# Seven block products for four of the eight tile pairs in batch 2's input stage, with VectorE's work there in a new order

## The chip, the core and the metric

One core of a Trainium2 chip runs the whole program: no other core takes part, and there is one launch. The metric is the device time of one execution in microseconds (us). The kernel before was run three times: 207.71, 206.24 and 207.14, median 207.14. One execution was recorded by the hardware profiler; its own time is 205.84 us, and its span, from the first to the last instruction of the trace, is 204.10 us.

The engines are TensorE (PE in the profile, its weight loads PEld), VectorE (DVE), ScalarE (ACT), GpSimd (POOL) and SyncE (SP), which here only issues transfers. An issue of a transfer stands on the queue of the engine that makes it.

## The reference

Four batches of attention with eight heads, 768 tokens and 64 columns a head feed a layer of two matrix products. Each query sees the keys within 15 positions of its own, and 24 summaries: of each block of 32 keys the maximum, of each block of 32 values the mean, with log 32 added to their score.

```python
k_sum = k.reshape(B, H, nb, block, D).max(axis=3)      # B, H, S, D = 4, 8, 768, 64; block = 32
v_sum = v.reshape(B, H, nb, block, D).mean(axis=3)
scores_l = scale * q @ k.T                             # kept where |i - j| < 16
scores_s = scale * q @ k_sum.T + log(block)
a = softmax(concat([scores_l, scores_s]))
x = (a @ concat([v, v_sum])) -> (3072, 512)
h = x @ w_in                                           # w_in: 512 x 2048
g = h / (1 + exp(-1.702 * h))
out = g @ w_out                                        # w_out: 2048 x 512, out: 3072 x 512, float32
```

## The kernel before, in words

**Engines and order.** Each engine runs its instructions in the order in which the program writes them; the framework sets the semaphores between engines. So the order of the calls in the program is the order of each queue. All helpers record through one wrapper, so nearly every instruction of the profile has line 28, and tiles are told apart by their names.

**Stages.** A batch has 768 tokens, two halves of 384. Its *input stage* multiplies x (transposed, `xTT`, tile name `xT`) by w_in and applies the gelu on ScalarE into `gT`, 16 tiles of 128 of the 2048 middle columns by 768 tokens. Its *output stage* multiplies `gT` by w_out and writes tokens in groups of 128. Batch 0 goes through a lead of its own (the calls from line 920 on) and `ff_in`, `ff_out`; batches 1 and 2 through the loop at line 1124; batch 3 through the code from line 1171.

**Plain input products.** A tile is two halves of 384 columns; each is four matmuls of 128 x 128 by 384 (`ff_step`). The loop takes tiles in pairs j and j + 8, in the order `order2`. A pair is 16 matmuls.

**Seven block products.** The matrices are cut in 2 x 2 blocks, and sums of blocks replace eight block products by seven, in Strassen's manner. For the output stages of batches 1 to 3 `product(b, t, what)` (line 775) does this: `gs` holds four sums of blocks of `gT` (`g_sums`, line 683), `ws` four sums of blocks of w_out (`w_sum`); each `what` is eight matmuls of 256 columns that share a weight sum, and `keep_it` (799), `give` (806) and `store` (816) hold, add and write the results. The variable `seq` gives the order of the products. In the last group the last copy is cut in two, a VectorE half stored on SyncE's queue and a ScalarE half stored on its own.

For the input stage only batch 3 does this, for six of its eight pairs (`PLAIN = 2`). `win_sum` (716) makes four sums `wsi` of blocks of w_in, each 128 x 2048, and `x_sums` (725) four of x. `win_sum` is called four times on VectorE at the start of batch 2's input stage (line 1129). For a pair, `ff_product` (739) does product 1 to 7 of two matmuls each, `ff_copy` (757) moves partial sums between banks: "a" a VectorE copy of bank A into bank C, "s" a ScalarE copy of bank E, "b" and "c" VectorE sums of bank A with "s" into bank B and into bank E. `ff_gelu` (771) ends a bank. The table `steps` (1198) says in which of a pair's slots each is called; a new pair starts every seven slots, so neighbouring pairs overlap. The banks come from `last_bank` (733): three of A, one of B, two of C and two of E.

**The next batch's attention, beside.** During the input stage of batch b the keys, queries and values of batch b + 1 are made ready. Transfers: SyncE transposes keys (`xk`, line 567) and queries (`xq`, 574) by DMA, in pairs of heads; GpSimd issues the loads (`load_batch`, 246; `load_turned`, 123, called at 1146 for the next queries, behind a small GpSimd copy `gate2` that waits for x). `value_rows` (1077) sums the values' blocks: 48 small matmuls (`vsum`, 280) into `ps_vs`, then `block_sums` (304) on VectorE, then transfers to `vw`. `rest_k` (578), for each pair of heads, takes the maxima of the key blocks on VectorE into `ks`, then copies the halos (`key_halos`, 355) and the rows of maxima (`key_rows`, 349) into `kx`. During the output stage `beside` (1057) takes from the table `plan` (1038) by slot: "s" scores and their exponential, "m" mask, "v" values (601, with `norm`, 625: one reciprocal and one product for each of two banks), "d" the transposition of x by DMA (`dx`, 639, on SyncE's queue).

**The sums gs around batch 2.** After each pair of tiles in batch 1 and 2, `g_sums` makes the four sums of that pair on VectorE; two of the last pair's come after the first product of the output stage.

**The lead.** For batch 0, keys and queries are turned on TensorE. `q_turn` (401) writes the turned queries of two pairs of heads into two parts of one bank, and `q_copy` (407) takes them out, one pair on VectorE and one on ScalarE. `idle(n)` (298) is n matmuls whose results nobody reads. `v_sum` (483, first called at 970) sums the value blocks.

Of the kernel before, what the change touches and what calls it, by code (L numbers as in the profile page):

```python
# [35 lines left out]
def kernel(  # L36
# [311 lines left out]

    def key_rows(p, s, ks, eng=dve, j0=0):
# [228 lines left out]
    def rest_k(p, s, eng=dve):  # L578
        ks = attp.tile([128, nb], BF16, name="ks", tag="ks")
# [21 lines left out]
    def values(b, half, g):  # L601
# [19 lines left out]
        x2[g] = attp.tile([128, 2, JH, 2, D], F16, name="x2", tag="x2", bufs=4)  # L621
        for i in range(2):
            norm(x2[g][:, :, :, i].rearrange("p h j d -> p j h d") if b else x2[g][:, i], pvs[i])

    def norm(x, pv):
        rc = attp.tile([128, 2, JH, 1], F32, name="rc", tag="rc")
# [89 lines left out]
    def win_sum(what):  # L716
# [6 lines left out]
        dve.tensor_tensor(out=wsi[what], in0=a, in1=b_, op=op)  # L723
# [51 lines left out]
    def product(b, t, what):  # L775
# [40 lines left out]
        def store(o, tok, cols=slice(0, d_model)):  # L816
            r0 = b * S + tok
            sp.dma_start(out=out[r0:r0 + 128, cols], in_=now[t, o][:, cols])
# [117 lines left out]
    s_bias(1)  # L936
    q_turn(0)
# [4 lines left out]
    idle(6)  # L942
# [32 lines left out]
    av_edges(0)  # L975
# [148 lines left out]
    for b in range(1, B - 1):  # L1124
        nxt = b + 1 < B
        s = (b + 1) % 2
        if b == B - 2:
            for w in range(4):
                win_sum(w)
        for n in range(0, NT, 2):  # L1130
            if n == 0:
                ff_open(order2[0:4], (lambda: tx(1, 1)) if b == 1 else None)
            elif n == 2:
                for nt in order2[0:4]:
                    ff_one(1, nt)
                g_sums(0)
                g_sums(1)
            else:
# [3 lines left out]
                g_sums(n // 2, dve, (0, 1) if n + 2 == NT else (0, 1, 2, 3))  # L1142
            if nxt:
                if n == 0 and b > 1:
                    pool.tensor_copy(out=gate2, in_=xTT[1][1][:, 1, 0:1])
                    load_turned(q, b + 1, qb2, "qb")
                if n // 2 == 1:
                    value_rows(s)
                if n // 2 == 2 * b:
                    xq(0, s)  # L1150
                    xq(1, s)
                if n // 2 in (2, 3, 4, 5):
                    rest_k(n // 2 - 2, s)
        if nxt:
            exp_soon()
            beside(b + 1, -1)
        i = 0
        for t, what in seq:
            product(b, t, what)
            if i == 0:  # L1160
                g_sums(NT // 2 - 1, dve, (2, 3))
            if nxt:
# [9 lines left out]
    for ab in (True, False):  # L1172
        plast[ab] = ctx.enter_context(tc.tile_pool(name=f"plast{ab:d}", bufs=2, space=bass.MemoryType.PSUM))
    b, n = B - 1, NT // 2
    PLAIN = 2

    def plain(nt, half, tag):
        ph = last_bank(tag, "ph")[:, 0:HALF]
        ff_step(ph, half, nt)
        gelu(half, nt, ph)  # L1180

    def ff_do(j, what):
        if isinstance(what, int):
            ff_product(j, what)
        elif what in "asbc":
            ff_copy(j, what)
        elif what == "g":
            g_sums(j, pool, (0, 1))
        else:
            ff_gelu(j, what)  # L1190

    for i, tag in enumerate("CCEEAAA"):
# [3 lines left out]
        if i in (5, 6):  # L1196
            g_sums(0, pool, (0, 1) if i == 5 else (2, 3))
    steps = {0: [1, "a"], 1: [5, "s"], 9: [7, "c"], 10: [3], 4: [2], 5: [6, "b"], 13: [4],
             6: ["C"], 11: ["B"], 12: ["E"], 14: ["A"], 15: ["g"]}
# [20 lines left out]
    q_ = slice(PLAIN, n)  # L1220
# [35 lines left out]
```

## Time and profile before

| what | value |
|---|---|
| runs (us) | 207.71, 206.24, 207.14; median 207.14 |
| the profiled execution (us) | 205.84, its span 204.10 |
| granted TensorE clock, mean over the span | 0.995 |
| instructions in the span | 5864 |
| HBM read, written | 27.26 MB, 6.29 MB |
| largest group | 416 matmuls of `ph`, 128x384: 70.2 us |
| second largest | 104 ScalarE gelus into `gT`, 128x384: 49.8 us, 491 ns each |

The profile's page is read from the top. The first part gives each engine's busy time and its share of the span; the chain of waits follows the end of the program back to what released each step, and so tells which engine the time is made of; the groups of instructions give the mean duration of one. A view of stretches of time cuts these by stage, and the timeline gives single instructions: their start in us from the start of the span, their duration, engine, operation, output and inputs, and in brackets the idle time ahead of them with what ended it. The stages of the profiled execution, by the first and last matmuls of each: batch 1's input stage from 74.2 to 96.05, its output stage to 118.6; batch 2's input stage to 140.05 and output stage to 162.6; batch 3's to 183.4 and 204.1.

### The profile page before, as it was taken

The page shows a single profiled execution, that of the slowest core. Times are in us where ns is not written, and L with a number is a line of the kernel's source. Part 1 is how long each engine was busy: PE and PEld are TensorE (multiplying, and loading weights), DVE is VectorE, ACT ScalarE, POOL GpSimd, SP SyncE. Part 2 cuts the span into 40 slices and gives each one's busy share as a digit, 9 for nine tenths or more (in the row PEclk, how much of TensorE's full clock was granted, in tenths as well). Part 3 has the DMA queues.
Part 4 walks back from the last instruction along what each step waited for, and adds up shares of the span by engine and source line. Part 5 has one row for each costly group of instructions (what it writes and reads, how often), then busy time and mean ns, then how long its engine had stood idle before and what let it go on. Part 6 is the DMA issues. An engine that isn't in the chain of part 4 may idle for free.

```text
span 204.1 us, 5864 instructions
## 1 busy us (share of the span) xinstructions
PE 197.2 (97%) x2364; PEld 137.0 (67%) x2364; DVE 139.1 (68%) x387; ACT 125.9 (62%) x241; POOL 92.1 (45%) x143
## 2 busy tenths in 40 slices
PE   7999999999999999999999999999999999999991
PEld 6567554556664666566888866657888865578881
DVE  6666876585854974897767698996759446757221
ACT  4686874549777617777771546778651578982220
POOL 7965489446999691002965054000000029990000
PEclk9999999999999999999999999999999999999997
DMA  5999999999999999999999979995024920000232
GB/s 171 173 166 204 208 209 219 180 154 240 111 155 150 189 181 126 168 177 104 145 206 132 178 125 152 125 245 131 17 89 111 158 94 3 0 0 3 103 118 89
DMA packets 96138, 28.13 MB, mean 138 GB/s; under 512 B 83680, under 2 KB 93296, under 8 KB 96112
## 3 DMA queue, kind: packets, MB, share of 16 engines
q0 software_dynamic: 69648, 13.24, 85.4%
q1 hardware_dynamic: 26320, 14.46, 34.0%
q8 instruction: 18, 0.29, 0.6%
q14 instruction: 8, 0.07, 0.1%
q10 hardware_dynamic: 144, 0.07, 0.1%
HBM read 27.26 MB, written 6.29 MB: 164 GB/s over the span
## 4 chain that ended last, share of the span: by engine, by line
PE 92%; ACT 3%; DMA 2%; DVE 1%; issue 0%; SPq 0%; DVEq 0%
PE ph L28 33%; PE poA L28 16%; PE po L28 11%; PE poB L28 8%; PE ps_av L28 4%; PE ps_s L28 4%; PE poC L28 4%; PE phA L28 4%; DMA gT<-in_k_dram 2%; PE ps_t L28 1%; PE ps_x L28 1%; PE phB L28 1%; PE phC L28 1%; ACT a_sb L28 1%; PE ps_vt L28 1%; PE phE L28 1%
## 5 line engine op out<-in xcount | busy, mean ns | idle before, releaser
L28 PE MATMUL ph<-xT,w_in_sb 128*128 128x384 f16 x416 | 70.2, 326 | 0.1
L28 PEld LDWEIGHTS <-w_in_sb 128*128 128x128 f16 x452 | 43.7, 98 | 27.8 <-issue 0.2
L28 ACT ACTIVATE gT<-ph 128x384 f16<-128x384 f32 x104 | 49.8, 491 | 18.5 <-PE ph L28 18.2
L28 PEld LDWEIGHTS <-gT 128*128 128x128 f16 x312 | 28.8, 98 | 11.0
L28 ACT ACTIVATE a_sb<-ps_s 128x768 bf16<-128x768 f32 (+1 forms) x32 | 25.0, 826 | 10.8 <-PE ps_s L28 10.8
L28 PEld LDWEIGHTS <-gs 128*128 128x128 f16 x288 | 27.7, 98 | 3.4
L28 POOL DMA_DIRECT2D vw<-in_v_dram x36 | 24.5, 701 | 11.5 <-DMA kb<-in_k_dram 4.2
L28 POOL TENSOR_TENSOR gs<-gT 128x384 f16<-128x384 f16 x9 | 8.2, 909 | 42.4 <-ACT gT L28 42.4
L28 PE MATMUL po<-w_out_sb,gT 128*128 128x512 f16 x96 | 23.6, 380 | 0.0
L28 DVE TENSOR_TENSOR a_sb<-a_sb,mk 128x768 bf16<-128x768 bf16 x28 | 14.9, 554 | 6.5 <-ACT a_sb L28 5.9
L28 PE MATMUL poA<-ws,gs 128*128 128x256 f16 x144 | 18.7, 273 | 0.0
L28 DVE TENSOR_TENSOR x<-ps_av,rc 128x384 f16<-128x384 f32 x32 | 17.8, 557 | 1.1
L28 DVE TENSOR_TENSOR gs<-gT 128x384 f16<-128x384 f16 (+1 forms) x34 | 13.4, 393 | 7.2 <-ACT gT L28 6.9
L28 POOL DMA_DIRECT2D qb<-in_q_dram x16 | 15.1, 961 | 1.8 <-DMA w_in_sb<-in_moe_w_in_dram 1.3
L28 PEld LDWEIGHTS <-kx 64*128 64x128 bf16 (+1 forms) x372 | 9.4, 95 | 6.8 <-issue 4.4
L28 POOL DMA_DIRECT2D kb<-in_k_dram x14 | 13.6, 991 | 0.3 <-issue 0.3
L28 DVE TENSOR_REDUCE ks<-kx 128x24 bf16<-128x768 bf16 x12 | 11.4, 948 | 3.4 <-ACT kx L28 3.2
L28 ACT ACT_TABLE_LOAD x10 | 12.8, 1283 | 1.0 <-PEq L1240 0.8
L28 ACT ACTIVATE osb<-poA 128x256 f32<-128x256 f32 (+1 forms) x9 | 3.3, 372 | 16.2 <-PE poA L28 12.7
L28 ACT ACTIVATE s<-poA 128x256 f32<-128x256 f32 x11 | 4.2, 385 | 11.2 <-PE poA L28 11.2
L28 PEld LDWEIGHTS <-a_sb 128*64 128x64 bf16 (+2 forms) x400 | 7.9, 108 | 2.8 <-issue 1.3
L28 PE MATMUL poA<-w_out_sb,gT 128*128 128x256 f16 x72 | 9.4, 273 | 0.0
(119 smaller groups left out, 282.3 us busy)
## 6 DMA issues: line engine op xcount, KB each, us to landing
out_dram<-osb SPq DMA_DIRECT2D x22, 256.0 KB, 3.7
kb<-in_k_dram POOLq DMA_DIRECT2D x14, 192.0 KB, 7.1
qb<-in_q_dram POOLq DMA_DIRECT2D x12, 192.0 KB, 9.9
vw<-in_v_dram POOLq DMA_DIRECT2D x36, 64.0 KB, 5.5
w_out_sb<-in_moe_w_out_dram POOLq DMA_DIRECT2D x4, 512.0 KB, 13.0
w_in_sb<-in_moe_w_in_dram POOLq DMA_DIRECT2D x3, 512.0 KB, 12.6
vw<-vs SPq DMA_DIRECT2D x6, 198.0 KB, 5.8
gT<-in_k_dram SPq DMA_DIRECT2D x2, 384.0 KB, 3.6
```

Of the source, the lines that this page charges most:

```text
L28: r = f(*a, **kw)
```

## The change

- **Batch 2's input stage** (`in_seven`, line 1215 of the changed kernel) takes four pairs (j = 0 to 3) in the plain way and four (j = 4 to 7) by seven block products, with the same `steps`. One half of tiles 3 and 11 is put between the last pair's products. The second of the four pairs starts its product 1 and copy "a" at slot 2 of the stage, five slots sooner than its place. The banks A (three) and B (one) are now opened for batches 2 and 3 alike, C and E for each stage by itself; batch 2's output stage uses A and B, and a new pool `psb2` for the attention beside it. The block sums of values use the two E banks.
- **Sums of w_in.** Sums 0 and 2 go to GpSimd, after the output products of batch 1 that have slots 9 and 10; sums 1 and 3 stay on VectorE at the start of batch 2.
- **Keys of batch 3.** The maxima are taken for two pairs of heads at a time (`key_max`): the first two pairs in one piece after `value_rows`, the other two in three parts, after slots 10, 17 and 24. Their halos (`key_halos2`) and rows (`key_rows2`) go to GpSimd. In batch 1's input stage the same is done on VectorE, two pairs at a time.
- **Sums of gT in batch 2.** Sums 0 and 1 of pairs 0 and 1 in one VectorE operation each; of pair 2 on GpSimd; sums 2 and 3 of pairs 0 and 1 on GpSimd after slots 3 and 6; sums 0 and 1 of pairs 4 to 6 on GpSimd by `steps`; of the last pair and of pair 3 on VectorE at the end. Sums 2 and 3 of pairs 2 to 7 are two VectorE operations of 128 x 2304 (`sums23`), after the first and the second output product. In batch 1 the sums of two pairs at a time are one operation each.
- **Queries of batch 3** (`xq`) are transposed after slot 8.
- **Values** of batches 2 and 3: one reciprocal and one product for the two banks.
- **The lead.** Each turned query has a bank of its own; two idle matmuls ahead of the first `q_turn` replace six behind it; the first value sums and the first own and edge products of values come sooner, and `s_bias(3)` later.
- **The tail.** The last copy is one ScalarE operation and one store on its queue.

The core of the diff:

```diff
     def vsum(s):
 
-        if s == 1 and not vs_ps[0]:
+        if plast:
+            ps = [last_bank("E", "ps_vs") for e in range(2)]
...
+    def key_max(g, s, part=0, parts=1):
+
+        flat = kxs[s].rearrange("p i t c -> p (i t c)")
+        o, n = 2 * g * NQ * 128, 2 * NJ // parts
+        if part == 0:
+            ks_of[g] = attp.tile([128, 2, nb], BF16, name="ks", tag="ks2", bufs=2)
+        dve.tensor_reduce(out=ks_of[g].rearrange("p i (j e n) -> p (i j) e n", e=2, n=2)[:, part * n:(part + 1) * n],
+                          in_=at(flat, o + 256 * n * part, [[256, n], [192, 2], [block, 2], [1, block]]),
+                          axis=AX.X, op=ALU.max)
...
+    def key_halos2(g, s, eng):
+        flat = kxs[s].rearrange("p i t c -> p (i t c)")
+        o, n = 2 * g * NQ * 128, 2 * NJ
+        eng.tensor_copy(out=at(flat, o + 256 + 96, [[256 * NJ, 2], [256, NJ - 1], [1, 16]]),
...
     def q_turn(p):
-        if p % 2 == 0:
-            st["Q2"] = pturn.tile([128, 1024], BF16, name="ps_q", tag="turn")
-        st["Q", p] = st["Q2"][:, p % 2 * HALF:p % 2 * HALF + HALF]
+        st["Q", p] = pturn.tile([128, 1024], BF16, name="ps_q", tag="turn")[:, 0:HALF]
         turn_plain(st["Q", p], qe[:, 2 * p:2 * p + 2])
...
+            pv = ps.rearrange("p (i c) -> p i c", i=2)[:, :, 0:390].rearrange("p i (n c) -> p i n c", c=D + 1)
+            rc = attp.tile([128, 2, 2 * JH, 1], F32, name="rc", tag="rc2", bufs=2)
+            dve.reciprocal(out=rc, in_=pv[..., D:D + 1])
+            dve.tensor_mul(x2[g].rearrange("p h j i d -> p i (h j) d"), pv[..., 0:D],
+                           rc.to_broadcast([128, 2, 2 * JH, D]))
+            return
...
-    def g_sums(j, eng=dve, which=(0, 1, 2, 3)):
-
-        a1, a2 = gTb[:, j], gTb[:, j + NT // 2]
+    def g_sums(j, eng=dve, which=(0, 1, 2, 3), n=1):
+
+        j1, j2 = slice(j, j + n), slice(j + NT // 2, j + NT // 2 + n)
+        a1, a2 = gTb[:, j1], gTb[:, j2]
         l, r = slice(0, HALF), slice(HALF, S)
         for w in which:
-            a, b_, op = {0: (a1[:, r], a2[:, r], ALU.add), 1: (gs[:, 0, j], a1[:, l], ALU.subtract),
-                         2: (a1[:, l], a1[:, r], ALU.subtract), 3: (a2[:, l], gs[:, 1, j], ALU.subtract)}[w]
-            eng.tensor_tensor(out=gs[:, w, j], in0=a, in1=b_, op=op)
+            a, b_, op = {0: (a1[:, :, r], a2[:, :, r], ALU.add), 1: (gs[:, 0, j1], a1[:, :, l], ALU.subtract),
+                         2: (a1[:, :, l], a1[:, :, r], ALU.subtract),
+                         3: (a2[:, :, l], gs[:, 1, j1], ALU.subtract)}[w]
+            eng.tensor_tensor(out=gs[:, w, j1], in0=a, in1=b_, op=op)
 
     N1 = d_model // 2
...
-    def win_sum(what):
+    def win_sum(what, eng=dve):
...
+    def open_last(stack, b, tags):
+        for tag, n in tags:
+            plast[tag] = stack.enter_context(tc.tile_pool(name=f"last{tag}{b}", bufs=n, space=bass.MemoryType.PSUM))
+
     def last_bank(tag, name):
-        return plast[tag in "AB"].tile([128, 512], F32, name=name, tag="last" + tag,
-                                       bufs={"A": 3, "E": 2, "B": 1, "C": 2}[tag])
+        return plast[tag].tile([128, 512], F32, name=name, tag="last" + tag)
...
             now[t, bank] = (last_bank("B" if bank == "A" and t == 2 else {"A": "A", "B": "E", "C": "C"}[bank],
                                       "po" + bank) if b + 1 == B
-                            else pmm.tile([128, 512], F32, name="po" + bank, tag="mm"))
+                            else last_bank("B" if bank == "B" else "A", "po" + bank) if b + 2 == B
+                      else pmm.tile([128, 512], F32, name="po" + bank, tag="mm"))
         po = now[t, bank][:, 0:N1]
         for i in range(n):
...
         elif last:
-            for c, eng, queue in ((slice(0, 128), dve, sp), (slice(128, N1), act, act)):
-                copy(eng, now[t, "o2"][:, c], po[:, c])
-                queue.dma_start(out=out[b * S + HALF + t * 128:b * S + HALF + t * 128 + 128, c],
-                                in_=now[t, "o2"][:, c])
+            give("o2", lo, None)
+            store("o2", HALF + t * 128, lo, act)
         else:
...
     s_bias(1)
+    idle(2)
     q_turn(0)
     q_turn(1)
     q_copy(0, dve)
     q_copy(1, act)
     k_max(0)
-    idle(6)
...
     k_max(3)
     s_bias(2)
-    s_bias(3)
     s_own(2)
-    s_own(3)
     s_edges(2)
     s_exp(2)
+    s_bias(3)
+    v_sum((0,))
+    s_own(3)
     s_edges(3)
     s_exp(3)
-    v_sum((0,))
+    av_own(0)
+    av_edges(0)
     v_sum((1,))
     v_copy((0, 1), dve)
-    av_own(0)
     av_own(1)
-    av_edges(0)
...
+    def sums23(j0):
+        q_ = slice(j0, NT // 2)
+        yield dve.tensor_tensor(out=gs[:, 2, q_], in0=gTb[:, q_, 0:HALF], in1=gTb[:, q_, HALF:S], op=ALU.subtract)
+        yield dve.tensor_tensor(out=gs[:, 3, q_], in0=gTb[:, j0 + NT // 2:NT, 0:HALF], in1=gs[:, 1, q_],
+                                op=ALU.subtract)
...
+    def in_plain():
+        s = 0
...
-                g_sums(1)
+                g_sums(0, n=2)
...
+                if n // 2 in (3, 5):
+                    g_sums(n // 2 - 1, n=2)
...
+            if n // 2 in (2, 4):
+                rest_k2(n // 4 - 1, s)
...
+    def in_seven(b, first):
+
+        n, s = NT // 2, (b + 1) % 2
+        for w in (1, 3):
+            win_sum(w)
+        pool.tensor_copy(out=gate2, in_=xTT[1][1][:, 1, 0:1])
+        load_turned(q, b + 1, qb2, "qb")
+        for i, tag in enumerate("CCEEAAAB"):
+            plain((0, n, 1, n + 1)[i % 4], i // 4, tag)
+            if i == 3:
+                x_sums()
+        value_rows(s)
+        key_halos2(0, s, pool)
+        key_max(0, s)
+        key_rows2(0, s, pool)
+        for i, tag in enumerate("CCAA"):
+            plain(2 + n * (i % 2), i // 2, tag)
+        g_sums(0, dve, (0, 1), 2)
+        for i in range(2):
+            plain(3 + n * i, 0, "E")
+        g_sums(2, pool, (0, 1))
+        key_halos2(1, s, pool)
+        for slot in range(7 * (n - first)):
+            for j in range(first, n):
+                at_ = slot - 7 * (j - first)
+                if j == first + 1 and at_ in (0, -5):
+                    at_ = -1 if at_ == 0 else 0
+                for what in steps.get(at_, ()):
+                    ff_do(j, what)
+            if slot in (3, 6):
+                g_sums(slot // 3 - 1, pool, (2, 3))
+            if slot in (10, 17, 24):
+                key_max(1, s, slot // 7 - 1, 3)
+            if slot == 8:
+                xq(0, s)
+                xq(1, s)
+            if slot == 24:
+                key_rows2(1, s, pool)
+        last = n - 1
+        ff_do(last - 1, "A")
+        plain(3, 1, "C")
+        ff_do(last, 7)
+        ff_do(last, "c")
+        ff_do(last, 3)
+        ff_do(last - 1, "g")
+        ff_do(last, "B")
+        ff_do(last, "E")
+        plain(3 + n, 1, "E")
+        ff_do(last, 4)
+        ff_do(last, "A")
+        g_sums(last, dve, (0, 1))
+        g_sums(3, dve, (0, 1))
+
+    for b in range(1, B - 1):
+        seven = b == B - 2
+        if seven:
+            mid.close()
+            open_last(ctx, b, (("A", 3), ("B", 1)))
+            with ExitStack() as banks:
+                open_last(banks, b, (("C", 2), ("E", 2)))
+                in_seven(b, 4)
+            mid = ExitStack()
+            psb = mid.enter_context(tc.tile_pool(name="psb2", bufs=2, space=bass.MemoryType.PSUM))
+            bulk = sums23(2)
+        else:
+            in_plain()
+        exp_soon()
...
             if i == 0:
-                g_sums(NT // 2 - 1, dve, (2, 3))
-            if nxt:
-                beside(b + 1, i)
+                if seven:
+                    beside(b + 1, -1)
+                else:
+                    g_sums(NT // 2 - 1, dve, (2, 3))
+            beside(b + 1, i)
             i += 1
-            if nxt and b + 2 < B:
+            if b + 2 < B:
...
                     load_batch(b + 2)
                 if i in (16, 18):
                     xk(i // 2 - 8, b % 2)
+                if i in (9, 10):
+                    win_sum(2 * (i - 9), pool)
 
...
+    open_last(ctx, B - 1, (("C", 2), ("E", 2)))
```

More of the change, by code (lines that the diff above doesn't have):

```diff
@@ L280, in vsum @@
     def vsum(s):
-        if s == 1 and not vs_ps[0]:
+        if plast:
+            ps = [last_bank("E", "ps_vs") for e in range(2)]
+        elif s == 1 and not vs_ps[0]:
             ps = [pmm.tile([128, 512], F32, name="ps_vs", tag="mm") for e in range(2)]
@@ L625, in norm @@
     def norm(x, pv):
[L626 removed]
+        rc = attp.tile([128, 2, JH, 1], F32, name="rc", tag="rc", bufs=4)
         dve.reciprocal(out=rc, in_=pv[..., D:D + 1])
@@ L722, in win_sum @@
                      2: (a11, a21, ALU.subtract), 3: (a12, wsi[1], ALU.subtract)}[what]
-        dve.tensor_tensor(out=wsi[what], in0=a, in1=b_, op=op)
+        eng.tensor_tensor(out=wsi[what], in0=a, in1=b_, op=op)
     def x_sums():
@@ L731, with plain, ff_do @@
     plast = {}
+    def open_last(stack, b, tags):
+        for tag, n in tags:
+            plast[tag] = stack.enter_context(tc.tile_pool(name=f"last{tag}{b}", bufs=n, space=bass.MemoryType.PSUM))
     def last_bank(tag, name):
-        return plast[tag in "AB"].tile([128, 512], F32, name=name, tag="last" + tag,
-                                       bufs={"A": 3, "E": 2, "B": 1, "C": 2}[tag])
+        return plast[tag].tile([128, 512], F32, name=name, tag="last" + tag)
+    def plain(nt, half, tag):
+        ph = last_bank(tag, "ph")[:, 0:HALF]
+        ff_step(ph, half, nt)
+        gelu(half, nt, ph)
+    def ff_do(j, what):
+        if isinstance(what, int):
+            ff_product(j, what)
+        elif what in "asbc":
+            ff_copy(j, what)
+        elif what == "g":
+            g_sums(j, pool, (0, 1))
+        else:
+            ff_gelu(j, what)
+    steps = {0: [1, "a"], 1: [5, "s"], 9: [7, "c"], 10: [3], 4: [2], 5: [6, "b"], 13: [4],
+             6: ["C"], 11: ["B"], 12: ["E"], 14: ["A"], 15: ["g"]}
     ff_now = {}
@@ L814, in product, with store @@
         last = b == B - 1 and t == JH - 1
-        def store(o, tok, cols=slice(0, d_model)):
+        def store(o, tok, cols=slice(0, d_model), queue=sp):
             r0 = b * S + tok
-            sp.dma_start(out=out[r0:r0 + 128, cols], in_=now[t, o][:, cols])
+            queue.dma_start(out=out[r0:r0 + 128, cols], in_=now[t, o][:, cols])
             if not last:
@@ L1123 @@
     halves[0] = True
[L1124 to L1129, printed above, removed]
+    def sums23(j0):
[5 more added lines that the diff above has]
+        s = 0
         for n in range(0, NT, 2):
             if n == 0:
-                ff_open(order2[0:4], (lambda: tx(1, 1)) if b == 1 else None)
+                ff_open(order2[0:4], lambda: tx(1, 1))
             elif n == 2:
@@ L1141 @@
                         ff_one(half, nt)
-                g_sums(n // 2, dve, (0, 1) if n + 2 == NT else (0, 1, 2, 3))
-            if nxt:
[L1144 to L1153, printed above, removed]
@@ new lines @@
+    for b in range(1, B - 1):
[12 more added lines that the diff above has]
+        exp_soon()
+        if not seven:
@@ L1219 @@
     product(b, 2, 1)
-    q_ = slice(PLAIN, n)
-    dve.tensor_tensor(out=gs[:, 2, q_], in0=gTb[:, q_, 0:HALF], in1=gTb[:, q_, HALF:S], op=ALU.subtract)
-    dve.tensor_tensor(out=gs[:, 3, q_], in0=gTb[:, PLAIN + n:2 * n, 0:HALF], in1=gs[:, 1, q_], op=ALU.subtract)
+    for _ in sums23(PLAIN):
+        pass
     for t in range(JH):
```

47 lines of the change are left out of this document (25 added, 22 removed).

## The prediction

> **What bounds the kernel now.** I read the page's busy shares and its chain of waits, then the busy times by stage, then the timeline at the places that the change touches, last the transfers of single issues.
>
> ```profile
> PE 197.2 (97%) x2364; PEld 137.0 (67%) x2364; DVE 139.1 (68%) x387; ACT 125.9 (62%) x241; POOL 92.1 (45%) x143
> PE 92%; ACT 3%; DMA 2%; DVE 1%; issue 0%; SPq 0%; DVEq 0%
> 0.00:19.50 19.50, 17.10 (x343) 13.12 (x344) 12.47 (x42) 12.60 (x21) 14.81 (x23) 1.00 1.44 178
> 118.60:140.05 21.45, 21.45 (x181) 12.78 (x180) 19.58 (x57) 15.25 (x32) 5.04 (x5) 1.00 1.48 174
> 162.60:183.40 20.80, 20.74 (x135) 12.93 (x133) 12.03 (x23) 17.22 (x40) 15.72 (x18) 1.00 0.09 29
> ```
>
> The last three rows are stages: length, then busy time of PE, weight loads, DVE, ACT and POOL, then clock, DMA share, GB/s. TensorE is 92% of the chain. It stands 2.4 us in the first 19.5 and not at all in batch 2's input stage (118.60 to 140.05), where VectorE's 19.58 us are work that nobody waits for. So an edit gains what it takes from TensorE, and loses what it makes TensorE wait.
>
> **Products.** A plain pair is 16 matmuls, a pair by seven products 14. Four pairs: 8 matmuls fewer, each 15.71 / 96 = 0.164 us: -1.31, all on the path.
>
> ```profile
> 118.61 5.20 PE ph L28 x32
> 123.81 0.53 PE ps_vs L28 x48
> 124.34 15.71 PE ph L28 x96
> 169.21 0.57 DVE L28 TENSOR_TENSOR phB<-phA,vw 128x384 f32<-128x384 f32 x1 [1.05 <-PE phA L28]
> 169.69 0.56 DVE L28 COPY phC<-phA 128x384 f32<-128x384 f32 x1
> 169.83 0.48 PE L28 MATMUL phA<-vw,kx 128*128 128x384 f16 x2
> 170.35 0.57 DVE L28 TENSOR_TENSOR phE<-phA,vw 128x384 f32<-128x384 f32 x1
> ```
>
> Batch 3 shows the new coupling: product 7 starts (169.83) 0.05 after VectorE's sum (169.21 + 0.57), so TensorE now depends on three VectorE operations a pair, 1.70 us in the 2.29 of 14 matmuls; ScalarE holds the same load there (17.22 of 20.80).
>
> On the clock of the kernel before: TensorE does eight plain tiles to 123.81, the value sums to 124.34, six tiles to 128.27, then product 1. VectorE starts at 118.19:
>
> ```profile
> 118.19 1.22 DVE L28 TENSOR_TENSOR kx<-w_in_sb 128x2048 f16<-128x2048 f16 x1
> L28 DVE TENSOR_TENSOR vw<-xT,xT 128x768 f16<-128x768 f16 x2 | 1.1, 554 | 0.0
> 125.58 0.28 DVE L28 COPY vpart<-ps_vs 128x128 f32<-128x128 f32 x1
> 125.90 1.18 DVE L28 TENSOR_TENSOR vs<-ps_vs,vpart 32x128 bf16<-32x128 f32 x4
> 134.02 0.94 DVE L28 TENSOR_REDUCE ks<-kx 128x24 bf16<-128x768 bf16 x1
> ```
>
> Two sums of w_in (2.44) and four of x (2.2) end near 122.9, inside the wait for 124.34. Then 0.28 + 1.18 + 1.88 (maximum of two pairs, at most twice 0.94) + 1.1 (two sums over 768 columns, as the row of 554) reach 129.0. The first copy ends at 129.5, and product 2 could have run at 129.25; the sum before product 7 comes 0.37 late. I take 0.6 of standing (0 if the short operations overlap fully, 1.0 if each is late by 0.5). In the steady part a third of a maximum (0.94 x 512/768 = 0.63) joins the 1.70: 2.33 against 2.29, three times, at most 0.15, taken as nothing.
>
> **The keys' wait, which decides.** Pairs 2 and 3 of batch 3's keys were reduced at 134.02. In the new order a third of that stands on VectorE after the first pair's last sum, near 131.8, in front of the sum for product 7 of the second pair. It reads what the fourth key transposition writes:
>
> ```profile
> 118.53 6.11 SPq L28 DMA_TRANSPOSE kx<-kb  x4
> 122.71 1.94 SPq L28 DMA_TRANSPOSE kx<-kb  x1
> kx<-kb SPq DMA_TRANSPOSE x1, 10.3
> SPq L28 <- DMA kx<-kb: 1.5, 1, 1.5
> 133.05 0.59 SPq L28 DMA_DIRECT2D vw<-vs  x1
> ```
>
> Issued at 122.71, it takes 10.3 us and lands at 133.0; the SP queue's wait for it ends at 133.05. Nothing before it on SP or in its data moves. So VectorE waits from 131.8 to 133.1, adds 0.6, then the sum (0.57): product 7 starts at 134.3. TensorE, 13 products further, came there at 133.2. It stands 1.1. From there 38 matmuls remain (6.2): the stage ends near 140.5 instead of 140.05. **+0.45**, of which -1.31 is the products' gain. Bounds: -0.7 if the keys are there in time (-1.31 + 0.6), +1.5 if they land a microsecond later.
>
> **GpSimd.** It takes two sums of w_in, key copies, and sums of gT.
>
> ```profile
> L28 POOL TENSOR_TENSOR gs<-gT 128x384 f16<-128x384 f16 x9 | 8.2, 909 | 42.4 <-ACT gT L28 42.4
> L28 POOL COPY kx<-kx 128x80 bf16<-128x80 bf16 x8 | 1.8, 260 | 0.0
> L28 POOL COPY kx<-ks 128x288 bf16<-128x288 bf16 x4 | 1.7, 434 | 0.0
> 106.52 3.39 POOL L28 DMA_DIRECT2D vw<-in_v_dram  x5 [0.40 <-PE poB L28]
> 119.67 1.04 POOL L28 CAST gate<-xT 128x1 bf16<-128x1 f16 x1 [9.76 <-DMA xT<-x]
> ```
>
> A sum over 2048 columns has no row: at most 0.909 x 2048/384 = 4.85, at least 4.0 with the copies' fixed part taken off (260 at 80 columns, 434 at 288: 0.19). I take the upper end. Two of them fill 109.91 to 119.6, the idle 9.76 before the gate at 119.67, so the four loads of q behind the gate do not move; were they 1 us longer, those loads would start 1.7 later. In the input stage the halo copies of pairs 2 and 3 wait for the same transposition to 133.3; behind them stand eight sums, two copies and the sum that the second output product needs: 1.1 + 8 x 0.91 + 0.8 + 0.91 = 143.4 at the latest, 143.1 where sums overlap. TensorE reaches that matmul after a product, two score groups and six matmuls, 2.4 us behind the stage's end: 142.9. **+0.4** (0 to 0.65).
>
> **The lead.** Each turned query has a bank, so ScalarE's copy no longer waits for VectorE's:
>
> ```profile
> 7.72 0.56 DVE L28 COPY qT<-ps_q 128x384 bf16<-128x384 bf16 x1 [1.64 <-PE ps_q L28]
> 8.31 0.49 ACT L28 ACTIVATE qT<-ps_q 128x384 bf16<-128x384 bf16 x1 [0.75 <-DVE qT L28]
> 52.75 2.05 POOL L28 DMA_DIRECT2D qb<-in_q_dram  x2
> qb<-in_q_dram POOLq DMA_DIRECT2D x1, 192.0 KB, 5.4
> 59.22 0.47 PEld L28 LDWEIGHTS <-qb 128*128 128x128 bf16 x6 [0.18 <-DMA qb<-in_q_dram]
> ```
>
> The copy at 8.31 can start at 7.72, six idle matmuls become two, and the first value sums fill a wait: some 0.4 us by 18 us. It is not kept. The last q transfer (the second of the two from 52.75, so issued near 53.8, + 5.4 = 59.2) lands as its weight load starts, 59.22, after a wait named for it. GpSimd's issues there follow earlier transfers, not TensorE. An earlier TensorE waits longer: **0** (-0.5 if all is kept, 0 at the other end, since no work is added).
>
> **The tail.** The last copy ran in halves, ScalarE's behind VectorE's:
>
> ```profile
> 200.07 0.29 DVE L28 COPY osb<-poA 128x128 f32<-128x128 f32 x1 [0.45 <-PE poA L28]
> 200.39 0.28 ACT L28 ACTIVATE osb<-poA 128x128 f32<-128x128 f32 x1 [3.43 <-DVE osb L28]
> 200.70 0.37 ACTq L28 DMA_DIRECT2D out_dram<-osb  x1
> L28 ACT ACTIVATE osb<-poA 128x256 f32<-128x256 f32 x8 | 3.1, 384 | 12.7 <-PE poA L28 12.7
> ```
>
> One ScalarE copy (0.38) from 200.07 issues at 200.48, 0.22 sooner; the store is twice as large. **-0.15** (-0.22 to +0.1).
>
> **At nothing:** pairing the key work and the sums in batch 1, and one reciprocal and product for two banks. They shorten VectorE's queue behind TensorE's full stages; if they gave a wait it would be under one such operation, 0.5. The order of the transposes of x stays behind an output store, so an earlier x moves none.
>
> **Sum:** +0.45 + 0.4 - 0.15 = +0.7. The profiled execution took 205.84 (span 204.10 and 1.74 around it), 1.30 below the median of the runs, 207.14. The sum is put on the median: **207.8**. About 1% (2.07 us) is what a measurement of this kernel can tell from no change.
>
> **Rivals.**
> *Keys in time.* The fourth transposition lands before 131.8, since q's loads or stores stand otherwise in the queues. For it: 10.3 us is one sample, taken among q's loads. Against: those loads and the queues before it are the same. Then -1.31 + 0.6 - 0.15 = -0.9: 206.3.
> *Slower: VectorE and GpSimd hold each other up at the hand-over to the output products.* There VectorE has four sums over 384 columns and two over 2304, all from SBUF, while GpSimd is at its last sums.
>
> ```profile
> 182.74 0.91 POOL L28 TENSOR_TENSOR gs<-gs,gT 128x384 f16<-128x384 f16 x1
> 183.18 0.68 DVE L28 TENSOR_TENSOR gs<-gT 128x384 f16<-128x384 f16 x1 [0.66 <-ACT gT L28]
> 184.17 1.35 DVE L28 TENSOR_TENSOR gs<-gT 128x2304 f16<-128x2304 f16 x1
> L28 DVE TENSOR_TENSOR gs<-gT 128x384 f16<-128x384 f16 x33 | 12.0, 364 | 7.2 <-ACT gT L28 6.9
> ```
>
> The one place that shows both has VectorE at 0.68 where the group's mean is 0.36. If each waits for the other's whole operation, GpSimd's last sum comes up to 4 x 0.36 + 1.35 = 2.8 later, and TensorE with it: +0.7 + 2.8 = +3.5, 210.6. It decides (over 1%) once the long sum gets in front of GpSimd's last one, 1.4 lost. Against: VectorE reaches that long sum only after a copy that waits for TensorE. The Trainium skill states this rule on "SBUF — State Buffer", section "Who interferes with whom": a VectorE instruction with two SBUF inputs contends with a GpSimd instruction that reads SBUF, and the later one fully blocks. By that rule the sum would be 210.6; the row of 0.68 agrees in direction, and one row does not show how often it happens.
> *The lead is kept* beside keys in time: -0.9 - 0.4 = -1.3: 205.8.
>
> **How the numbers follow.** Forecast 0.42; keys in time 0.22; VectorE against GpSimd 0.29; lead kept 0.07. Faster by over 1% (below 205.07) needs the last case and no standing at the start: 0.06. Slower by over 1% (above 209.21): most of the contention case and a little of keys landing over a microsecond late: 0.30. Within: 0.64. The range takes in the lead's case with 0.3 less standing (205.5) and ends at the contention's own value, 210.6, which leaves out half of that case; the forecast's own range is 206.8 to 209.0.
>
> **What would show it.** Right: the first maximum over 512 columns idles about 1.3 us for the key transposition and TensorE stands about 1.1 us at that place; the first gs matmul group stands a few tenths for GpSimd; the w_in sums on GpSimd take 4.0 to 4.85; the weight load at 59.22 waits longer for its transfer than 0.18. Wrong: no wait for keys; sums of 384 columns on VectorE doubled at 140 to 143 us; TensorE 0.4 us earlier still at 60.

## The result, and the profile after

The kernel before took 207.00 us (median of 16 executions, 205.95 to 207.71), the changed one 210.41 (16 executions, 207.43 to 219.63). The ratio is 1.0104, interval 1.0073 to 1.0134; every ratio here leaves out the executions over 1.5% above the fastest of their kernel, which are six of 16 for the changed kernel, five of ten for e3 and four of ten for e4, and what those are is told below. In ten of the 16 the granted clock was 0.976 to 0.992; the other six, at 0.999 or 1.000, have a median of 208.2. The profiled execution is the fastest, 207.43 us with a span of 205.70.

First the busy shares and the chain of waits by engine, from the page of the changed kernel.

```profile
PE 196.9 (96%) x2352; PEld 136.2 (66%) x2352; DVE 135.5 (66%) x324; ACT 127.1 (62%) x245; POOL 114.7 (56%) x167
PE 89%; DVE 4%; issue 2%; ACT 2%; DMA 2%; DVEq 0%
```

TensorE has less work, but its share of the chain falls from 92% to 89%: VectorE (4%) and "issue" (2%, time in which TensorE waited for nothing that the profile shows) now hold it up. The view by stage (length, then busy time of PE, weight loads, DVE, ACT, POOL) says where:

```profile
119.60:140.60 21.00, 20.44 (x171) 12.12 (x169) 16.56 (x29) 15.99 (x36) 17.54 (x25) 1.00 1.36 176
140.60:165.15 24.55, 22.98 (x362) 19.19 (x360) 18.70 (x35) 12.40 (x22) 2.18 (x3) 1.00 0.37 77
```

Batch 2's input stage is 21.00 long where it was 21.45, its output stage 24.55 where it was 22.55. The main waits of TensorE that the kernel before does not have (us in total, times, longest):

```profile
PE ps_av L28 <- issue: 0.9, 1, 0.9
PE poA L28 <- DVE s L28: 0.8, 1, 0.8
PE poB L28 <- DVE gs L28: 0.7, 1, 0.7
PE phA L28 <- DVE phB L28: 0.4, 1, 0.4
PE phC L28 <- DVE phC L28: 0.2, 1, 0.2
```

Batch 2 begins at 119.62 instead of 118.61 (+1.0: 0.7 up to the first input product of the lead, which holds the first wait, and 0.3 before batch 1), its input stage gives back 0.45, its output stage costs 2.0, and from the last matmul to the end it is 3.08 (202.62 to 205.70) where it was 4.03 (200.07 to 204.10): -0.95. That is +1.6, the difference of the spans.

### The profile page after: what moved, and what is told of

The parts are those of the page before. It is cut to its first block, busy times and chain, and to the rows that moved or that the text cites. A ratio compares the mean times of both kernels' runs of the same rounds, so it can differ in the third digit from the quotient of the medians.

```text
span 205.7 us, 5819 instructions
## 1 busy us (share of the span) xinstructions
PE 196.9 (96%) x2352; PEld 136.2 (66%) x2352; DVE 135.5 (66%) x324; ACT 127.1 (62%) x245; POOL 114.7 (56%) x167
## 4 chain that ended last, share of the span: by engine, by line
PE 89%; DVE 4%; issue 2%; ACT 2%; DMA 2%; DVEq 0%
PE ph L28 28%; PE poA L28 15%; PE po L28 11%; PE poB L28 7%; PE phA L28 6%; PE ps_av L28 5%; PE ps_s L28 4%; PE poC L28 3%; DVE gs L28 2%; PE phC L28 2%; PE phB L28 2%; DMA gT<-in_k_dram 2%; PE ps_t L28 1%; PE ps_x L28 1%; PE phE L28 1%
## 5 line engine op out<-in xcount | busy, mean ns | idle before, releaser
L28 PE MATMUL ph<-xT,w_in_sb 128*128 128x384 f16 x352 | 60.2, 326 | 0.1
L28 PEld LDWEIGHTS <-w_in_sb 128*128 128x128 f16 x412 | 39.7, 98 | 25.6 <-issue 0.6
L28 ACT ACTIVATE gT<-ph 128x384 f16<-128x384 f32 x88 | 42.3, 491 | 15.3 <-PE ph L28 14.5
L28 POOL DMA_DIRECT2D vw<-in_v_dram x36 | 24.6, 707 | 11.4 <-DMA kb<-in_k_dram 5.3
L28 POOL TENSOR_TENSOR gs<-gT 128x384 f16<-128x384 f16 x15 | 13.7, 916 | 26.8 <-ACT gT L28 26.8
L28 DVE TENSOR_TENSOR x<-ps_av,rc 128x384 f16<-128x384 f32 (+1 forms) x24 | 16.6, 691 | 0.8
L28 DVE TENSOR_TENSOR gs<-gT 128x768 f16<-128x768 f16 (+2 forms) x16 | 10.2, 638 | 7.7 <-ACT gT L28 7.7
L28 ACT ACT_TABLE_LOAD x10 | 12.8, 1283 | 1.0 <-PEq L1354 0.8
L28 DVE TENSOR_REDUCE ks<-kx 128x24 bf16<-128x768 bf16 (+2 forms) x10 | 11.1, 1109 | 3.5 <-ACT kx L28 3.2
L28 ACT ACTIVATE osb<-poA 128x256 f32<-128x256 f32 x9 | 3.4, 383 | 15.8 <-PE poA L28 15.8
L28 POOL TENSOR_TENSOR gs<-gs,gT 128x384 f16<-128x384 f16 x11 | 10.0, 909 | 0.9
L28 PE MATMUL poB<-ws,gs 128*128 128x256 f16 x72 | 9.5, 273 | 0.7 <-DVE gs L28 0.7
## 6 DMA issues: line engine op xcount, KB each, us to landing
w_in_sb<-in_moe_w_in_dram POOLq DMA_DIRECT2D x3, 512.0 KB, 12.6
```

Source lines behind the costliest of these rows:

```text
L28: r = f(*a, **kw)
```

## The experiments

All are compared with the kernel before by ratio, and with both traces by place.

**Hand-over to the output products.** The timeline of the changed kernel there:

```profile
140.60 0.50 DVE L28 TENSOR_TENSOR gs<-gT 128x384 f16<-128x384 f16 x1 [0.66 <-ACT gT L28]
140.86 1.01 POOL L28 TENSOR_TENSOR gs<-gT 128x384 f16<-128x384 f16 x1
141.14 0.95 DVE L28 TENSOR_TENSOR gs<-gs,gT 128x384 f16<-128x384 f16 x1
141.95 0.91 POOL L28 TENSOR_TENSOR gs<-gs,gT 128x384 f16<-128x384 f16 x1
142.01 1.06 DVE L28 TENSOR_TENSOR gs<-gT 128x384 f16<-128x384 f16 x1
143.11 0.36 DVE L28 TENSOR_TENSOR gs<-gs,gT 128x384 f16<-128x384 f16 x1
143.13 0.72 PE L28 MATMUL poB<-ws,gs 128*128 128x256 f16 x5 [0.73 <-DVE gs L28]
...
145.32 1.35 DVE L28 TENSOR_TENSOR gs<-gT,gs 128x2304 f16<-128x2304 f16 x1
146.58 0.41 DVE L28 COPY s<-poA 128x256 f32<-128x256 f32 x1
...
147.05 1.03 PE L28 MATMUL poA<-ws,gs 128*128 128x256 f16 x8 [0.83 <-DVE s L28]
```

Two readings. VectorE's sums take 0.95 and 1.06 while GpSimd has its own, and 0.36 once GpSimd is done; each of the two ends 0.2 behind GpSimd's sum, while GpSimd's own keep 0.91 to 1.01. And the copy of s, which the product at 147.05 waits for, stands behind the second long sum.

e3: `copy(dve if t == 0 and b + 1 < B else act, t_, po)` becomes `b + 2 < B`.

> The changed kernel with the three copies of partial output products of batch 2's first token group on ScalarE instead of VectorE. Theory one: TensorE's 0.83 us at the second ws product come from a copy that stands on VectorE between the two sums over 2304 columns (1.35 us each); with the copies on ScalarE that standing falls below 0.2, and the time by 0.7 to 0.8. Theory two: the sums themselves are what the products wait for; then a standing of about the same length remains, named for gs, and the time stays.

Measured: ratio 0.9976 (0.9945 to 1.0007). The wait for s is gone, and the output stage a full 1.0 shorter; the other wait remains:

```profile
143.74 0.72 PE L28 MATMUL poB<-ws,gs 128*128 128x256 f16 x5 [0.82 <-DVE gs L28]
```

Theory one held for this wait; the ratio, over five of ten executions, does not size the gain.

e4: `ff_do(last - 1, "g")` becomes `g_sums(last - 1, dve, (0, 1))`.

> The changed kernel with the sums 0 and 1 of pair 6 on VectorE instead of GpSimd, ahead of those of the last pair. Theory one, contention: VectorE's sums over 384 columns took 0.95 and 1.06 us while GpSimd had its own; without those all of VectorE's at the end take 0.36 to 0.5, and TensorE's 0.73 us ahead of the first product with sums fall below 0.3, the time by 0.4 to 0.7. Theory two, VectorE has simply too much to do after the last gelu: two sums more make the standing longer by 0.5 to 0.7.

Measured: ratio 1.0067 (1.0033 to 1.0101); in the trace the standing at poB is gone although VectorE has two sums more. Its last ones, after GpSimd's last copy has ended at 141.76:

```profile
140.71 1.05 POOL L28 COPY kx<-ks 128x288 bf16<-128x288 bf16 x2
141.40 0.57 DVE L28 TENSOR_TENSOR gs<-gT 128x384 f16<-128x384 f16 x1
142.00 0.36 DVE L28 TENSOR_TENSOR gs<-gs,gT 128x384 f16<-128x384 f16 x1
142.28 0.35 DVE L28 TENSOR_TENSOR gs<-gT 128x384 f16<-128x384 f16 x1
142.66 0.36 DVE L28 TENSOR_TENSOR gs<-gs,gT 128x384 f16<-128x384 f16 x1
```

So it was contention and not VectorE's load. From the first output product to batch 3's first input product it is 23.49 here and 24.52 in the changed kernel. The ratio does not show this gain: its executions spread from 207.06 to 218.33, as those of the changed kernel do.

**The lead.** e2 gives the changed kernel the old lead; e1 gives the kernel before the new lead and the new tail.

> The changed kernel with the lead of the kernel before. If the new lead costs what the trace of after shows (1.0 us at the start of batch 2's input stage), this is 0.7 to 1.0 faster than the changed kernel. The keys: in the trace of after TensorE came to batch 2 one us later than before and the fourth key transposition landed 1.4 sooner (8.9 instead of 10.3 us). If the keys were in time because of that, a wait of VectorE for the transposition, up to 1.3 us, appears at the first maximum over 512 columns here, and the gain is less. If they are in time anyway, no wait is there.

> The kernel before with only two parts of the change: the lead's new order with a bank for each turned query, and the last copy as one ScalarE operation and one store. Theory one, the trace of after is typical: from the last matmul to the end 3.1 us where the kernel before has 4.0, so -0.9; the lead has TensorE standing at about 13.8 us for nothing that the profile shows, and its first ph matmuls are 0.7 later: ratio about 0.999. Theory two, that standing is chance, and the lead's gain is lost at the q transfer near 59 us, as forecast: about -0.9 in all, ratio 0.996. Theory three, the lead's gain of 0.4 lasts: ratio 0.994.

Measured: e2 1.0026 (0.9990 to 1.0061), 206.23 to 208.52, the clock at 0.999 or 1.000 in all 8; e1 1.0011 (0.9979 to 1.0042). The new lead costs, in part through falls of the clock that e2 does not have. In e1 the tail's 0.5 to 0.9 is about used up by it: theory one. In e2 the keys were there when VectorE came, but GpSimd's halos waited 0.8 for them, so only just.

The place of the first input product alone does not size the lead, as TensorE's first matmuls vary by themselves. Here are the second group of key matmuls and the first input product in the kernel before (two lines of its chain of waits), in a second trace of it (e9, below) and in the changed kernel (lines of the timeline):

```profile
6.18 0.53 PE ps_k L28 x12
18.70 0.48 PE ph L28 x2
7.10 0.53 PE L28 MATMUL ps_k<-wide,kb 128*64 128x128 bf16 x12
19.51 0.48 PE L28 MATMUL ph<-xT,w_in_sb 128*128 128x384 f16 x2
5.95 0.53 PE L28 MATMUL ps_k<-wide,kb 128*64 128x128 bf16 x12
19.42 0.49 PE L28 MATMUL ph<-xT,w_in_sb 128*128 128x384 f16 x2
```

From one to the other it is 12.52 and 12.41 with the old lead and 13.47 with the new one (13.27 to 13.53 in e1, e3 and e4), so the new lead takes about 1.0 longer.

The standing for "issue": the changed kernel, and what moved on the instruction queue from 12.0 to 12.2 us.

```profile
14.76 0.18 PE L28 MATMUL ps_av<-v0n,a_sb 32*32 32x65 bf16 x1 [0.93 <-issue]
```

```profile
q8 instruction: 1, 0.02, 35.4%
```

The page counts 18 such packets; TensorE has 4704 instructions, some 260 a packet if all 18 are its own. In e1 the packet began at 12.8 to 13.0 and the standing ended at 15.53, in e3 at 12.4 to 12.6 and it ended at 15.01: 2.4 to 2.8 after the packet each time. Three kernels test whether that is the cause: e5 keeps only the banks and idle matmuls of the new lead, e6 only its order, e7 is the changed kernel with `idle(20)` for `idle(36)`.

> The changed kernel with only the first half of its lead: a bank for each turned query and two idle matmuls in place of six; the order of the value sums and products is that of the kernel before. What is open: TensorE stood 0.7 to 1.0 us for nothing named, in all four kernels with the new lead, at the end of the first edge products of values, and in each the standing ended 2.6 to 2.7 us after the one instruction packet of TensorE's queue began to move (12.1 and 14.76, 12.8 and 15.53, 12.4 and 15.01). Theory one, TensorE runs out of instructions there: it comes to the end of what is loaded before the next packet is in. With the old order it again waits for ScalarE's exponential and copies until then, so the standing is under 0.3. Theory two, the banks cause it: it stays at 0.7 to 1.0.

> The changed kernel with only the second half of its lead: value sums and first value products sooner; one bank for two turned queries and six idle matmuls as in the kernel before. Theory one, instructions run out: TensorE is as early as in the changed kernel, less the 0.4 of the query copies, so it still stands 0.3 to 1.0. Theory two, the banks: no standing. On the granted clock: it fell below 0.993 in 10 of 16 executions of the changed kernel and in 3 of 10 of the kernel with the new lead and tail alone, in none of 8 with the old lead; if the fewer idle matmuls let it fall, it stays above here and falls in the other half's kernel; if the standing does, it goes with the standing.

> The changed kernel with 20 idle matmuls at the start in place of 36, in a stretch where TensorE waits for keys anyway, so that everything after has a place 32 instructions sooner in TensorE's queue. Theory one, instructions run out at a fixed place of the queue: the standing moves 16 matmuls later in the program, into the value products after the second value sums, and keeps about its length. Theory two, a wait for data or a bank: it stays at the end of the first edge products. On the granted clock: fewer matmuls ahead of the first keys may let it fall more often.

```profile
15.27 0.91 PE L28 MATMUL ps_av<-v0n,a_sb 128*128 128x65 bf16 x29 [1.15 <-issue]
```

```profile
15.08 0.25 PE L28 MATMUL ps_av<-v0n,a_sb 32*32 32x65 bf16 x5 [0.48 <-issue]
```

```profile
15.34 0.54 PE L28 MATMUL ps_vt<-v0n,E 128*128 128x64 bf16 x12
15.72 0.26 PE L28 MATMUL ps_av<-v0n,a_sb 128*128 128x65 bf16 x3
16.29 0.39 PE L28 MATMUL ps_av<-v0n,a_sb 128*128 128x65 bf16 x5 [0.31 <-issue]
```

These are e5, e6 and e7. In e7 the standing is 16 matmuls later in the program (before the fourth matmul behind twelve sums, where it was before the last edge product); in e6, with four idle matmuls more, four earlier. It is a fixed place in TensorE's queue: in all ten traces that show the standing 223 matmuls lie ahead of it, and it ends 2.4 to 2.7 after that packet begins. So it is not a wait for data: I conclude that TensorE runs out of instructions and stands until the packet is in. The old lead is not free of it. In e12 (below), which has the old lead, the standing is there at the same 223:

```profile
15.06 0.19 PE L28 MATMUL ps_vt<-v0n,E 128*128 128x64 bf16 x1 [0.39 <-issue]
```

In the first trace of the kernel before the packet begins at 11.4 and TensorE comes to this place near 14.1, 2.7 later, so just late enough: what the new lead gains ahead of it is lost there. My expectation for e5 was wrong: it stands 1.15 although the order is the old one, as the queries alone bring TensorE there early enough. Its ratio is 1.0055 (1.0021 to 1.0088), e6's 1.0034 (1.0001 to 1.0067). e7 took 208.16, 217.80, 218.34 and 218.81, and has no ratio.

e11 is the kernel before with `idle(20)`.

> The kernel before with 20 idle matmuls at the start in place of 36. The changed kernel with this edit fell below 0.985 of the clock in 3 of 4 executions. If idle time of TensorE in the lead is what lets the clock fall, it falls here too (time 209 or more); if it takes the new order of the lead, this runs at 0.995 or more and near 207.

Measured: 209.46 and 209.53, ratio 1.0118 (1.0062 to 1.0174); clock 1.000 and 0.997; its trace stands 0.9 for issue as well, and its first input product comes at 21.32. So the time is that of the first case and the clock that of the second: in these two executions fewer idle matmuls did not let the clock fall, and they cost 2.5 all the same.

**Two traces again.** e9 is the kernel before, e10 the changed kernel.

> The kernel before, unchanged, for a second trace. The changed kernels all take 0.3 to 0.5 us more than the first trace of before between the q transfer near 59 us and batch 1's input stage. If the change causes that, this trace has 14.74 us there again, as the first has; if the first trace was a lucky one, about 15.05. From the last matmul to the end the first trace has 5.10 us from the start of the last product, the new tail 4.16 to 4.63: 5.1 again if the tail's gain is real.

> The changed kernel, unchanged, for a second trace, if possible of an execution in which the granted clock falls (10 of 16 so far below 0.993, in steps of 0.008: 0.992, 0.984, 0.976). Theory one: the clock falls to a half in whole windows, each some 3.3 us long (0.008 x 208 / 0.5), in the lead, where TensorE stands. Theory two: it falls where all engines are busy at once, in batch 2's input stage. If the clock stays at 1.0 here, the trace only repeats that TensorE stands 0.7 to 1.0 us at the end of the first edge products.

e9 took 207.72, and has 15.34 us at the place in question, so the 0.3 before batch 1 is chance and not the change. Its end is 5.12 after the start of the last product, so the tail's gain is real.

e10 took 218.24, and the place is neither of the two that I named. The timeline and, below it, the stages (the third number from the end is the clock):

```profile
108.95 9.68 DVE L28 TENSOR_TENSOR a_sb<-a_sb,mk 128x768 bf16<-128x768 bf16 x1
110.08 4.12 POOL L28 TENSOR_TENSOR kx<-w_in_sb 128x2048 f16<-128x2048 f16 x1
114.10 4.10 POOL L28 TENSOR_TENSOR kx<-w_in_sb 128x2048 f16<-128x2048 f16 x1
120.15 0.87 PE L28 MATMUL ps_av<-vw,a_sb 128*64 128x65 bf16 x24 [6.28 <-DVE x L28]
```

```profile
113.50:117.00 3.50, 0.37 (x4) 0.09 (x1) 3.50 (x1) 0.00 (x0) 3.50 (x2) 1.00 0.00 0
117.00:120.40 3.40, 0.25 (x10) 0.25 (x12) 3.33 (x6) 0.38 (x1) 1.20 (x1) 0.50 0.00 0
120.40:123.80 3.40, 3.14 (x57) 2.44 (x52) 3.33 (x7) 0.00 (x0) 0.00 (x0) 0.50 0.61 148
123.80:126.00 2.20, 2.20 (x22) 1.97 (x21) 0.35 (x1) 1.02 (x3) 0.00 (x0) 1.00 1.18 150
```

The last mask product of the output stage of batch 1, 0.56 otherwise, ends 0.43 behind GpSimd's two sums of w_in (118.20). TensorE waits 6.28 for what VectorE owes it, its clock is halved from 117.0 to 123.8, and 3.4 us of work in it cost 1.7 more: 8 of the 10.8 us over the profiled execution. In the profiled execution of the changed kernel the same two come apart:

```profile
107.60 0.56 DVE L28 TENSOR_TENSOR a_sb<-a_sb,mk 128x768 bf16<-128x768 bf16 x1
110.28 8.14 POOL L28 TENSOR_TENSOR kx<-w_in_sb 128x2048 f16<-128x2048 f16 x2
```

There the mask product was done 2.1 before the sums; it would have been done 0.6 before in e10, where TensorE was 1.35 later. The other VectorE work beside the sums reads a bank of matmul results (PSUM) and has its usual times (0.41, 0.96).

So the sums of w_in can cost 8 us. What decides whether they do is not shown. The counts point at the lead: a mean clock of 0.974 to 0.992 was seen in 10 of 16 executions of the changed kernel, in 8 of 20 of e3 and e4, in 3 of 4 of e7, in 3 of 20 with half of the new lead (e5, e6), in none of 30 with the old one (e2, e8, e12). But the time between the mask product's end and the sums is no shorter in the other traces with the new lead or half of it (2.1 to 2.8) than in those with the old one (1.6 to 2.7). One trace shows the mechanism; no other execution with a fallen clock is traced. e1, without sums of w_in on GpSimd, had a clock of 0.991 or less in 3 of 10 as well; its cause stays open.

**Mended.** e8 is the changed kernel with the old lead and the edits of e3 and e4; e12 besides moves sums of pair 0:

```diff
         key_max(0, s)
+        g_sums(0, pool, (0, 1))
         key_rows2(0, s, pool)
...
-        g_sums(0, dve, (0, 1), 2)
+        g_sums(1, dve, (0, 1))
```

> The changed kernel with the lead of the kernel before, the three copies on ScalarE and pair 6's two sums on VectorE. If the parts add: batch 2's input stage 0.5 below the kernel before, its output stage level, the end 0.9 sooner, no fall of the clock: 1.4 below, ratio 0.993. If ScalarE's copies now stand behind its exponentials, or the two sums come too late, about 0.5 of it stays with TensorE: 0.996.

> The kernel with the old lead and both hand-overs mended, and besides that the sums 0 and 1 of pair 0 on GpSimd in a stretch where it waits, so that VectorE comes 0.5 sooner to the first seven products. If the 0.6 us that TensorE stands there are VectorE's queue, 0.3 to 0.5 of them go: ratio 0.994 or less against the kernel before. If VectorE and GpSimd hold each other up there, VectorE's maximum of 1.75 us grows and nothing is gained.

Measured: e8 0.9963 (0.9933 to 0.9992), 204.79 to 206.61; e12 0.9943 (0.9914 to 0.9973), 204.76 to 207.68. Both beat the kernel before, by less than 1%; which of the two is better is not settled. e8 came out as the second case of its expectation: its trace still stands 0.4 ahead of the first product with gs.

This is not shown to be a gain of the block products. From batch 2's first input product to batch 3's, e8's trace takes 44.65, the two traces of the kernel before 44.01 and 44.48; from there to the end it takes 40.72 where they take 41.64 and 41.66. By these single traces, e8's being of its slowest execution, its gain is that of the tail; the kernel before with the new tail alone was not run. e12's edit takes away the 0.17 of standing ahead of the first pair's second product and leaves the 0.39 ahead of its seventh, so that part was not VectorE's queue. The trace of e12, its slowest execution, shows the wait for the keys that I had forecast:

```profile
132.38 0.57 DVE L28 TENSOR_TENSOR phE<-phA,vw 128x384 f32<-128x384 f32 x1 [0.58 <-PE phA L28]
134.75 0.69 DVE L28 TENSOR_REDUCE ks<-kx 128x16 bf16<-128x512 bf16 x1 [1.80 <-DMA kx<-kb]
135.35 0.56 DVE L28 TENSOR_TENSOR phB<-phA,vw 128x384 f32<-128x384 f32 x1
135.96 0.48 PE L28 MATMUL phA<-vw,kx 128*128 128x384 f16 x2 [1.67 <-DVE phB L28]
```

## Why the prediction was right, and where not

The time lay 2.6 above the forecast, inside the range by 0.2, and the direction was right. The reason given first was not what cost it, and two of the prediction's own signs of being wrong are there: no wait for keys, and VectorE's sums of 384 columns at 0.95 and 1.06. That the median is inside the range is in part luck. The upper end, 210.6, stood for contention at the hand-over, and that cost 0.7; what lifts the median from 208.2 to 210.4 is the executions with a fallen clock, which the prediction does not have.

- **Products:** -1.31 and 0.6 of standing; measured -0.45 for the stage, with 0.56 standing and 0.3 more of busy time, whose cause is not shown. Right in kind, 0.3 short.
- **The keys' wait, +1.1:** not there in this trace. The last transposition was issued at 122.64, no later than before, and took 8.9 and not 10.3; batch 2, and VectorE with it, came 1.0 later (below, the time from issue to landing, and what GpSimd and VectorE did when the keys were in):

```profile
kx<-kb SPq DMA_TRANSPOSE x1, 8.9
131.95 1.02 POOL L28 COPY kx<-kx 128x160 bf16<-128x160 bf16 x3
133.02 0.68 DVE L28 TENSOR_REDUCE ks<-kx 128x16 bf16<-128x512 bf16 x1
```

VectorE's 133.02 is 132.0 on the clock of the kernel before, so its queue was sized well (131.8). Even 10.3 would have been over at 132.9, in time by 0.1. The step that failed is the assumption that both sides of this wait keep their places: the transposition's length was 7.0 to 11.4 in twelve traces, and here its issue did not move with batch 2. The wait exists (0.47 in e8, 1.80 in e12), so it should have been a case with a chance and not the step that decides. The rival "keys in time" left the hand-over out of its sum, and its 206.3 did not come either.
- **Hand-over, +0.4:** 2.0. The rival "VectorE and GpSimd hold each other up" is what happened (e4), but it was VectorE that was held, by 0.7 at the product, and not GpSimd's last sum by 2.8. Beside it is a wait that the prediction did not have: VectorE's copies of s queue behind the long sums (e3). I had named what precedes the long sums on VectorE, and not what stands behind them.
- **Sums of w_in on GpSimd:** the duration was right (4.10 and 4.12, between 4.0 and 4.85), and the gate came no later (119.64). But I asked only what the sums delay on GpSimd, and not which VectorE work lies beside them. That cost is 0 in the profiled execution and 8 in e10. The Trainium skill's rule ("SBUF — State Buffer", "Who interferes with whom"), which I weighed for the hand-over only, is the one that speaks against this edit. The 9.68 agree with it in that the product stands while GpSimd has its sums; they differ in the order, since by the rule the first to issue goes on, and by the trace the product had begun first. The measurement decides.
- **The lead, 0:** +0.7 in the trace, about 1.0 counted from the keys. The q transfer, which was to swallow a gain, never came to bear: there was no gain, as TensorE ran out of instructions.
- **The tail, -0.15:** -0.95; the copy in one piece explains 0.2. I had the larger store land later; it landed sooner. In both traces of the kernel before the end comes 3.0 after ScalarE's last store is issued, in the changed one 2.3; why is not settled.

## What to carry to other kernels

Before idle GpSimd is given work, list what VectorE does beside it with both operands in SBUF, and how many microseconds lie between the two from one execution to the next: here 1.6 to 2.8 did no harm in nine traces and 0.6 cost 8 us in a tenth. A stretch of many short matmuls can be bound by the loading of instructions, so making it wait less for data may gain nothing. When several edits go in together, trace what each place gained: here the best kernels may owe their gain to the tail alone. When sums of blocks are added to an engine, look for the short copies that queue behind them.

## What the runs showed of the hardware

- In ten traces TensorE stood 0.3 to 1.5 with 223 matmuls of the program behind it, and the standing ended 2.4 to 2.7 after a packet of the instruction queue had begun, while the lead's loads were moving.
- VectorE's product of two operands in SBUF, which by the trace had begun 1.13 before GpSimd's first sum, stood through both sums, 8.12 us, with no turn between them. Why it did not end first is not shown: GpSimd was issuing transfers when it began, but it was in the profiled execution too, where the product took 0.56.
- VectorE's sums of 384 columns took 0.95 and 1.06 beside GpSimd's sums of the same size, and 0.36 without; GpSimd's took 0.91 to 1.01 there and 0.91 elsewhere.
- The clock was 0.50 from 117.0 on, 3.1 us after TensorE's last matmul had ended (113.9), and stayed so for 6.8. The Trainium skill's page "TensorE: Matmul & The Clock Gate", Part 1, has the half rate after an idle window of about 3.4 us; the trace is near it, with 3.1.
